# Group 8 of a linear recurrence loaded as one transfer per pair of sequences, and a drain without unread matmuls

## The chip, the cores and the metric

The kernel runs on one core of a Trainium2 chip. The metric is the device time of one execution in microseconds. A profile of one execution is shown beside the times; lines such as L252 are lines of the kernel's file. A core has a matrix engine (TensorE, PE in the profile), a vector engine (DVE), a scalar engine (ACT), GpSimd (POOL) and SyncE (SP), which issues most transfers. Transfers are moved by 16 DMA engines, which all issuers share.

## The reference

Four sequences of 5056 tokens with 256 channels go through a gated recurrence, and its output, taken as 20224 tokens, through a soft mixture of 8 experts with 4 slots each:

```python
sig = 1 / (1 + exp(-f_logit)); f = lower_bound + (1 - lower_bound) * sig
for t in range(S):                      # S = 5056, for each of B = 4 sequences
    h = f[:, t] * h + (1 - f[:, t]) * x[:, t]
    y[:, t] = h
logits = y.reshape(N, D) @ phi          # N = 20224, D = 256, 32 slots
slot_input = softmax(logits over tokens).T @ y
slot_out[e] = relu(slot_input[e] @ w1[e]) @ w2[e]      # F = 1024, 8 experts
out = softmax(logits over slots) @ slot_out
```

All inputs and the output are float32. Inputs f_logit and x are 20.7 MB each, w1 and w2 8.4 MB each, and the output is 20.7 MB.

## The kernel before

**Tiling.** The tokens of each sequence are cut into ten groups of G = 512. A unit is one group of one sequence, so there are 40. Groups 0 to 7 hold the first 4096 tokens. Group 9 is the last 512 tokens of the sequence, and group 8 (`odd` in the code) is what lies between: 448 tokens. Groups 2 to 7 are "long": there the two units of a pair are two successive groups of one sequence, loaded as one transfer of eight tokens on each of 128 partitions. In groups 0, 1, 8 and 9 the two units of a pair are the same group of two sequences. Units 32 to 35 are group 8: 32 and 33 are its first pair of sequences, 34 and 35 the second.

**One unit.** `load` brings f_logit into `f_t` and x into `x_t` (three buffers each, one pair in each buffer). `gate` (L241, scalar engine) makes `s_t`, the sigmoid of -f_logit in bf16. `enter` (L252, GpSimd) multiplies it by x into `u_t` (four buffers). Two neighbouring bf16 channels are then moved together as one float32 number: `s_to_channels` and `u_to_channels` transpose `s_t` and `u_t` on TensorE into PSUM (`sp`, `up`), so that channels lie on partitions and time runs along the row. `decay` (scalar engine) makes the decay factors `a`, `scan` (L319, vector engine) runs the recurrence, `to_tokens` and `keep_tokens` turn the result back into `ht`. `logits`, `exps`, `weights_to_tokens` and `slots` do the slots' softmax and sums.

**Group 8.** Its 448 tokens are not 4 x 128. Each sequence of a pair loads 3 tokens on each of 128 partitions (R3 = 3, 384 tokens), and the remaining L = 64 tokens of the two sequences come together on 128 partitions, alternating, as the fourth column of the pair's first half. That makes three transfers per tensor and pair (L222 and L226). `to_channels` turns the fourth column with an identity whose columns are split by sequence (L261) and the three others with one transpose each (L264). In the long groups `half_to_channels` (L273) turns a unit from one half of the partitions, with eight transposes of 64 partitions.

**Order.** The order is written out by hand in a loop over the units n (`manual_schedule`). Loads are issued six units ahead on SP's queue, every second unit; SP waits there for the buffer. On GpSimd the product of unit n + 3 is followed by weight loads as the table `W_AT` says. Weights are read as float32 and written as bf16 by transfers that GpSimd issues (L137, L147). Three of 16 loads are issued before unit 31; the others stand behind the products of units 34 to 37 and 39:

```python
W_AT = {9: 1, 17: 1, 25: 1, 31: 1, 32: 1, 33: 2, 34: 3, 36: 6}
```

The load of the last expert's w2 is issued in three parts.

**Drain.** After the last unit come the last slots (L461), `slot_sb` (the copy at L596), the slot input (L600), the experts' hidden layer (L631 to L664), the experts 0 to 3, then each further expert with its row sums (L670, L399), and the last expert (L725 to L740). Between these stand 24 matmuls whose results nobody reads: `spin` (L152, two of 128 columns) and `narrow` (L157, ten of 32 columns), once after the last slots and once after the slot input. Then the output is made from the stored exponentials and the slot outputs and written in transfers of up to 2 MB.

Of the kernel before, what the change touches and what calls it, by code (L numbers as in the profile page):

```python
# [9 lines left out]
F32 = mybir.dt.float32  # L10
# [8 lines left out]
def kernel(  # L19
# [10 lines left out]
    nc = tc.nc  # L30
    B, S, D = x.shape
    E = moe_w1.shape[0]
    F = moe_w1.shape[2]
    NS = moe_phi.shape[1]
    SPE = NS // E
    P = 128
    DC = D // P
    FC = F // P
    R = 4
# [6 lines left out]
    def first(g):  # L46
        return g * G if g < n_grp - 1 else S - G

    def used(g):
        return first(g + 1) - first(g) if g < n_grp - 1 else G  # L50
# [2 lines left out]
        return used(g) // R  # L53

    odd = n_grp - 2
    R3 = used(odd) // P
    L = used(odd) - P * R3
    assert 2 * L == P

    wide_r = 4 * R  # L60
    n_blk = (S // (P * wide_r))
# [1 line left out]
    blocks.append((n_blk * P * wide_r, (S - n_blk * P * wide_r) // P))  # L63
    assert sum(P * n_r for _, n_r in blocks) + L == S


    consts = ctx.enter_context(tc.tile_pool(name="consts", bufs=1))
    ident_f = consts.tile([P, P], F32, name="ident_f")
# [52 lines left out]
    rrow = store.tile([P, n_grp * R, B], F32, name="rrow")  # L121
    left = store.tile([P, L, 2], BF16, name="left")
    nc.vector.memset(left, 0.0)
# [8 lines left out]
    w1_sb = [wts.tile([P, DC, F], BF16, name=f"w1_sb{e}") for e in range(E)]  # L132
# [14 lines left out]
                nc.gpsimd.dma_start(out=w2_sb[i - E][:, ds(f, k)], in_=w2_r[i - E][:, ds(f, k)])  # L147


    def spin(dst, k, w):  # L150
        for _ in range(k):
            nc.tensor.matmul(dst[:, ds(0, w)], w1_sb[0][:, 0, :P], w1_sb[0][:, 0, :w],  # L152
                             start=True, stop=True, skip_group_check=True)

    def narrow(dst, k):
        for i in range(k):
            nc.tensor.matmul(dst[ds(i % B * NS, NS), ds(0, D)], w1_sb[0][:, 0, ds(0, NS)],  # L157
                             w1_sb[0][:, 0, ds(0, D)], start=True, stop=True,
                             skip_group_check=True)

    W_AT = {9: 1, 17: 1, 25: 1, 31: 1, 32: 1, 33: 2, 34: 3, 36: 6}
    w_next = [0]
    ctx.enter_context(tc.manual_schedule())
# [4 lines left out]
    with tc.tile_pool(name="sp2", bufs=3) as sp2, \  # L168
# [9 lines left out]
        slot_bank = pslot.tile([P, 2, D], F32, name="slot_ps")  # L178
# [12 lines left out]
        xs, fs, sts, uts, pss, psus, hs, hps, hts, lgs, ets = ({} for _ in range(11))  # L191

        def long(n):
            return 2 * B <= n < n_unit - 2 * B

        def place(n):
            if long(n):
                t, j = divmod(n, 2 * B)
                return 2 * t + j % 2, j // 2
            return divmod(n, B)  # L200
# [9 lines left out]
        def load(n, k=2):  # L210
            for src, dst, tag in ((f_logit, fs, "f_t"), (x, xs, "x_t")):
                if n % 2 == 0:
                    dst[n // 2] = ld.tile([P, 2, R, D], F32, name=tag, tag=tag)
                t = dst[n // 2]
                if long(n):
                    g, b = place(n)
                    nc.sync.dma_start(
                        out=t.rearrange("p u r d -> p (u r) d"),
                        in_=src[b, ds(first(g), 2 * G)].rearrange("(p r) d -> p r d", r=2 * R))
                elif n // B == odd:  # L220
                    b, t0 = n % B, first(odd)
                    nc.sync.dma_start(  # L222
                        out=t[:, 0, R3],
                        in_=src[ds(b, 2), ds(t0 + P * R3, L)].rearrange("b t d -> t b d"))
                    for m in range(2):
                        nc.sync.dma_start(  # L226
                            out=t[:, m, ds(0, R3)],
                            in_=src[b + m, ds(t0, P * R3)].rearrange("(p r) d -> p r d", r=R3))
                else:
                    for m in range(n, n + k):  # L230
                        nc.sync.dma_start(out=t[:, ds(m % 2, 1)], in_=tokens(src, m, 1))  # L231

        def gate(n, k=2):
            if n % 2 == 0:
                sts[n // 2] = sp2.tile([P, 2, R, D], BF16, name="s_t", tag="s_t")
            s_t, f_t = sts[n // 2][:, ds(n % 2, k)], fs[n // 2][:, ds(n % 2, k)]
            if n // B == odd:
                m = (R + R3) * D
                s_t = s_t.rearrange("p u r d -> p (u r d)")[:, :m]
                f_t = f_t.rearrange("p u r d -> p (u r d)")[:, :m]  # L240
            nc.scalar.activation(s_t, f_t, ACT.Sigmoid, scale=-1.0)  # L241

        def enter(n):
            uts[n] = sup.tile([P, R, D], BF16, name="u_t", tag="u_t")
            s_t, x_t = sts[n // 2][:, n % 2], xs[n // 2][:, n % 2]
            if n == 0:
                for r in range(0, R, 2):
                    nc.vector.tensor_tensor(uts[n][:, ds(r, 2)], s_t[:, ds(r, 2)],
                                            x_t[:, ds(r, 2)], ALU.mult)
            else:  # L250
                r = R3 if n // B == odd and n % 2 else R
                nc.gpsimd.tensor_tensor(uts[n][:, :r], s_t[:, :r], x_t[:, :r], ALU.mult)  # L252

        def to_channels(n, ps, t, rest):
            t = t.bitcast(F32)
            if n // B == odd:
                flat = ps.rearrange("c p r -> c (p r)")
                sides = ident_f.rearrange("p (t u) -> p u t", u=2)
                v = flat[:, ds(0, P * R3)].rearrange("c (p r) -> c p r", r=R3)
                k = P * R3 - n % 2 * L  # L260
                nc.tensor.matmul(flat[:, ds(k, P)], rest.bitcast(F32), sides,  # L261
                                 is_transpose=True, start=True, stop=True)
                for r in range(R3):
                    nc.tensor.transpose(v[:, :, r], t[:, r], ident_f)  # L264
                return
            for r in range(R):
                nc.tensor.transpose(ps[:, :, r], t[:, r], ident_f)  # L267

        def half_to_channels(n, ps, t):
            k = ds(n % 2 * (P // 2), P // 2)  # L270
            v = ps.rearrange("c p r -> c (p r)").rearrange("c (p r) -> c p r", r=2 * R)
            for r in range(2 * R):
                nc.tensor.transpose(v[:, :, r], t(r)[k].bitcast(F32), ident_f[k, k])  # L273

        def s_to_channels(n):
            if n % 2 == 0:
                pss[n // 2] = psp.tile([P, 2, P, R], F32, name="sp", tag="sp")
            to_channels(n, pss[n // 2][:, n % 2], sts[n // 2][:, n % 2],
                        sts[n // 2][:, 0, R3])

        def u_to_channels(n):
            ps = psu.tile([P, P, R], F32, name="up", tag="up")
            if long(n):
                half_to_channels(n, ps, lambda r: uts[n - n % 2 + r // R][:, r % R])
            else:
                to_channels(n, ps, uts[n], uts[n - n % 2][:, R3])
            psus[n] = ps.rearrange("c p r -> c (p r)").bitcast(BF16).rearrange(
                "c (t o) -> c t o", o=DC)

# [116 lines left out]
        def left_over():  # L406
            for b in range(B):
                k = ds(b * NS, NS)
                nc.gpsimd.tensor_copy(left[k, :, b % 2], etall[k, ds(S - L, L)])

# [74 lines left out]
        for n in range(n_unit):  # L485
# [14 lines left out]
            else:  # L500
# [40 lines left out]
                if n == n_unit - 2:  # L541
                    tail = psp.tile([P, 2, G], F32, name="tail", tag="sp")
# [46 lines left out]
        late_weights()  # L589
        slots(odd)  # L590
        late_slots()
        spin(tail[:, 1], 2, D)
        narrow(tail[:, 1], 10)
        slot_sb = hpool.tile([P, G, DC], BF16, name="slot_sb", tag="h")
        slot_sb = slot_sb.rearrange("p t o -> p (t o)").bitcast(F32)[:, ds(0, D)]
        nc.vector.tensor_copy(slot_sb, slot_ps)  # L596
# [2 lines left out]
        for o in range(DC):  # L599
            nc.tensor.matmul(sin_ps[:, o], slot_v[:, o], rep[:, 0],  # L600
                             start=True, stop=True, skip_group_check=True)
        spin(slot_bank[:, 1], 2, D)
        narrow(slot_bank[:, 1], 10)

    with tc.tile_pool(name="ew", bufs=1) as ew, \
         tc.tile_pool(name="pm", bufs=2, space=PSUM) as pm, \
# [17 lines left out]
        for q in range(E // Q):  # L624
            hi = ew.tile([P, F], BF16, name=f"hi{q}")
            for k in range(2):
                hi_ps = (psu.tile([P, H], F32, name="hi_ps", tag="up") if q == 0 else
                         pbig.tile([P, H], F32, name="hi_ps", tag=f"hi_ps{k}"))
                for o in range(DC):
                    for j in range(Q):  # L630
                        nc.tensor.matmul(hi_ps[ds(j * NS, NS)], sin[:, o],  # L631
                                         w1_sb[q * Q + j][:, o, ds(k * H, H)],
                                         start=(o == 0), stop=(o == DC - 1),
                                         skip_group_check=True)
# [7 lines left out]
        for q in range(E // Q):  # L642
# [4 lines left out]
            if q == 0:  # L647
                nc.tensor.matmul(cs_ps, rep2, cs1, start=True, stop=True)
            k = Q if q == 0 else Q - 1
            s0 = q * Q * SPE  # L650
            src = ht_ps[:, :, ds(s0, SPE)]
            src = bass.AP(tensor=src.tensor, offset=src.offset,
                          ap=[list(src.ap[0]), [P, FC], [NS + SPE, k], [1, SPE]])
            dst = hid[:, :, q * Q, ds(s0, SPE)]
            dst = bass.AP(tensor=dst.tensor, offset=dst.offset,
                          ap=[list(dst.ap[0]), [(E - 1) * NS, FC], [NS + SPE, k], [1, SPE]])
# [6 lines left out]
            src = ht_ps[:, :, ds((Q - 1) * NS + s0, SPE)]  # L663
# [23 lines left out]
        for i in range(0, n_late, 2):  # L687
            g_ps = (pbig.tile([P, 2, 2, P], F32, name="g_ps", tag="hi_ps1") if i else
                    psu.tile([P, 2, 2, P], F32, name="g_ps", tag="up"))
            for k in range(2):  # L690
                nc.tensor.matmul(g_ps[:, k], hi_v[tail_b, FC - n_late + i + k], ex[tail_b],
                                 start=True, stop=True, skip_group_check=True)
# [21 lines left out]
        for i in range(len(blocks)):  # L714
            expert(Q + i)
            row_sums(i)
            if i < len(blocks) - 1:
                k = ds(i * wide_r, wide_r)
# [3 lines left out]
        k = len(blocks) - 1  # L722
# [3 lines left out]
        for fc in range(FC):  # L726
# [4 lines left out]
                             start=fc == FC - n_late,  # L731
                             stop=fc in (FC - n_late - 1, FC - 1),
                             skip_group_check=True)
# [152 lines left out]
```

## Time and profile before

| | |
|---|---|
| median of 3 runs | 197.5 us (197.47 to 197.64) |
| the profiled execution | 197.47 us, span 195.7 us |
| PE busy | 147.1 us (75%) |
| DVE busy | 143.5 us (73%) |
| ACT busy | 141.4 us (72%) |
| POOL busy | 101.3 us (52%) |
| SP's transfers (q1) | 62.13 MB, 76.4% of 16 DMA engines |
| GpSimd's transfers (q0), bytes written | 8.42 MB, 21.6% |
| HBM read, written | 58.23 MB, 20.71 MB |

The span runs from the first to the last instruction; the rest of the execution's time lies around it. Busy times of different engines overlap. The page cuts the span into 40 slices of 4.9 us, and a digit there is a share in tenths. Issues from SP and GpSimd are marked SPq and POOLq in lists of waits.

### The profile page before, as it was taken

Reading aid. Unit: us, or ns where it says so; the run is one execution under the profiler, and the core shown is the slowest. Engines: PE = TensorE matmul, PEld = TensorE weight load, DVE = VectorE, ACT = ScalarE, POOL = GpSimd, SP = SyncE. Lnnn points to the kernel's source line nnn. Section 1 sums busy time; section 2 is a strip of 40 time slices with the busy share of each in tenths; the row PEclk is TensorE's granted clock in tenths of the full one; section 3 lists DMA queues with packets and bytes.
Section 4 is the critical chain, followed back from the end, with each engine's and each line's share of the span. In section 5 each row is a group of like instructions: output and inputs, shape, how many; then the busy total and the mean of one; then the engine's idle time right before and its main releaser. Section 6 shows DMA issues by size and latency. Waiting matters only on the chain.

```text
span 195.7 us, 3272 instructions
## 1 busy us (share of the span) xinstructions
PE 147.1 (75%) x1204; PEld 103.8 (53%) x1204; DVE 143.5 (73%) x185; ACT 141.4 (72%) x200; POOL 101.3 (52%) x78
## 2 busy tenths in 40 slices
PE   0688598897989979898997978996797999910000
PEld 0477478675767758665785857465564434300000
DVE  2669869989799999999999999442377998910000
ACT  3688688799799998899998798334089999940000
POOL 2589578874998688884969977280030000000000
PEclk9999889999999999999999999999999655555555
DMA  4999999999999999999999999999949999999994
GB/s 199 418 421 419 427 425 424 429 427 361 379 427 425 401 332 425 429 414 308 402 420 395 270 225 213 214 214 214 167 175 425 431 417 435 435 445 432 435 432 174
DMA packets 14161, 70.75 MB, mean 362 GB/s; under 512 B 1585, under 2 KB 2866, under 8 KB 10178
## 3 DMA queue, kind: packets, MB, share of 16 engines
q1 hardware_dynamic: 11520, 62.13, 76.4%
q0 software_dynamic: 2624, 8.42, 21.6%
q8 instruction: 9, 0.15, 0.3%
q14 instruction: 6, 0.05, 0.1%
q10 hardware_dynamic: 2, 0.00, 0.0%
HBM read 58.23 MB, written 20.71 MB: 403 GB/s over the span
## 4 chain that ended last, share of the span: by engine, by line
PE 24%; DMA 21%; DVE 15%; POOL 10%; ACT 9%; issue 6%; SPq 2%; POOLq 1%; ACTq 0%
DMA x_t<-in_x_dram 12%; DVE h L319 11%; DMA w_t<-in_moe_w_dram 10%; PE op L821 8%; POOL u_t L252 8%; ACT oc L762 5%; PE hp L332 4%; PE up L273 3%; PE sp L267 3%; DVE ht L351 3%; SPq L231 2%; PE slot_ps L189 2%; PE lg L365 1%; POOL w_sb L147 1%; ACT s_t L241 1%
## 5 line engine op out<-in xcount | busy, mean ns | idle before, releaser
L252 POOL TENSOR_TENSOR u_t<-s_t,x_t 128x1024 bf16<-128x1024 bf16 (+1 forms) x39 | 82.5, 2131 | 21.8 <-ACT s_t L241 15.1
L319 DVE TENSOR_TENSOR_SCAN h<-a,h,up 128x512 bf16<-128x512 f32 (+1 forms) x72 | 86.8, 1252 | 4.4 <-PE up L273 2.1
L241 ACT ACTIVATE s_t<-f_t 128x2048 bf16<-128x2048 f32 (+2 forms) x23 | 38.3, 1668 | 6.4 <-DMA f_t<-in_f_logit_dram 6.4
L332 PE MATMUL hp<-ident_f,h 128*128 128x128 f32 (+1 forms) x160 | 29.6, 309 | 8.0 <-DVE ht L351 6.0
L332 PEld LDWEIGHTS hp<-ident_f,h 128*128 128x128 f32 (+1 forms) x160 | 23.2, 207 | 19.1 <-DVE ht L351 12.4
L267 PE MATMUL sp<-ident_f,s_t 128*128 128x128 f32 x144 | 22.3, 300 | 5.6 <-ACT s_t L241 3.8
L301 ACT ACTIVATE a<-sp,lbs 128x1024 f32<-128x1024 bf16 x24 | 25.5, 1115 | 0.6 <-PE sp L267 0.6
L762 ACT ACTIVATE oc<-op,rrow 128x256 f32<-128x256 f32 x62 | 24.2, 551 | 0.1
L821 PE MATMUL op<-slot_bd,etall 64*128 64x512 bf16 x62 | 22.8, 570 | 0.6 <-POOL slot_bd L751 0.2
L267 PEld LDWEIGHTS sp<-ident_f,s_t 128*128 128x128 f32 x144 | 18.0, 154 | 7.7 <-ACT s_t L241 4.6
L308 ACT ACTIVATE a<-sp,lbs 128x512 f32<-128x512 bf16 (+2 forms) x22 | 17.9, 859 | 4.7 <-PE sp L267 4.3
L758 DVE TENSOR_TENSOR oc<-op,rrow 128x512 f32<-128x512 f32 x31 | 19.7, 685 | 1.6 <-PE op L821 1.5
L273 PE MATMUL up<-ident_f,u_t 64*128 64x64 f32 x192 | 17.8, 230 | 2.2 <-POOL u_t L252 2.1
L273 PEld LDWEIGHTS up<-ident_f,u_t 64*128 64x128 f32 x192 | 14.0, 138 | 6.2 <-POOL u_t L252 2.8
L189 PE MATMUL slot_ps<-rep,ident_f 128*128 128x256 f32 x52 | 16.7, 415 | 0.0
L821 PEld LDWEIGHTS <-etall 64*128 64x128 bf16 x62 | 9.1, 154 | 13.4 <-issue 8.0
L351 ACT COPY ht<-hp 128x512 f32<-128x512 f32 (+1 forms) x20 | 11.7, 583 | 3.5 <-PE hp L332 3.4
L351 DVE COPY ht<-hp 128x512 f32<-128x512 f32 (+1 forms) x20 | 13.3, 667 | 0.8 <-PE hp L332 0.8
L319 DVE TENSOR_TENSOR_SCAN h<-a,up 128x512 bf16<-128x512 f32 x8 | 9.3, 1209 | 2.4 <-PE up L267 2.4
L267 PE MATMUL up<-ident_f,u_t 128*128 128x128 f32 x48 | 9.4, 327 | 0.5 <-POOL u_t L252 0.5
L365 PE MATMUL lg<-h,phi 128*32 128x512 bf16 (+1 forms) x80 | 9.4, 389 | 0.3 <-ACT et L389 0.2
L189 PEld LDWEIGHTS slot_ps<-rep,ident_f 128*128 128x128 f32 x52 | 8.3, 194 | 1.6 <-issue 0.6
(127 smaller groups left out, 141.9 us busy)
## 6 DMA issues: line engine op xcount, KB each, us to landing
f_t<-in_f_logit_dram SPq DMA_DIRECT2D x12, 1024.0 KB, 12.3
x_t<-in_x_dram SPq DMA_DIRECT2D x12, 1024.0 KB, 12.0
out_dram<-oc SPq DMA_DIRECT2D x6, 2048.0 KB, 14.1
w_sb<-in_moe_w_dram POOLq DMA_DIRECT2D x14, 512.0 KB, 11.0
f_t<-in_f_logit_dram SPq DMA_DIRECT2D x12, 512.0 KB, 8.4
x_t<-in_x_dram SPq DMA_DIRECT2D x12, 512.0 KB, 9.9
out_dram<-oc SPq DMA_DIRECT2D x4, 896.0 KB, 6.4
out_dram<-ob SPq DMA_DIRECT2D x1, 2048.0 KB, 9.7
```

Of the source, the lines that this page charges most:

```text
L189: nc.tensor.matmul(slot_bank[:, 1], ident_f, wide_rep, start=False, stop=False, skip_group_check=True)
L241: nc.scalar.activation(s_t, f_t, ACT.Sigmoid, scale=-1.0)
L252: nc.gpsimd.tensor_tensor(uts[n][:, :r], s_t[:, :r], x_t[:, :r], ALU.mult)
L267: nc.tensor.transpose(ps[:, :, r], t[:, r], ident_f)
L273: nc.tensor.transpose(v[:, :, r], t(r)[k].bitcast(F32), ident_f[k, k])
L301: nc.scalar.activation(a, sp[:, :, :, :, o], ACT.Identity, scale=nomlb[:, ds(o, 1)], bias=1.0)
L319: nc.vector.tensor_tensor_scan(h[:, :T, o], decays[n // 2, o][:, n % 2, :T], up[:, :T, o], hs[number(g - 1, b)][:, ds(used(g - 1) - 1, 1), ...
L332: nc.tensor.transpose(hp[:n_p, r], hw[:, :n_p, r], ident_f)
L351: copy(hts[g][:n_p, b].rearrange("p r d -> p (r d)").bitcast(F32), hps.pop(n)[:n_p].rearrange("p r c -> p (r c)"))
L758: nc.vector.tensor_tensor(ob, op, scale.broadcast_to(list(ob.shape)), ALU.mult)
L762: nc.scalar.activation(ob[:, i], op[:, i], ACT.Copy, scale=scale[:, i])
L821: nc.tensor.matmul(op.rearrange("p u d -> p (u d)"), ew[:, :, r], slot_bd[ds(j * 2 * NS, 2 * NS)].rearrange("s u d -> s (u d)"), start=Tru ...
```

## The change

Group 8 of a pair of sequences now comes in one transfer per tensor: seven tokens on each of 128 partitions, the first sequence on partitions 0 to 63 and the second on 64 to 127. The tile is read as one row of 7 x 256 numbers. `gate` covers the same 1792 numbers as before, and `enter` of the pair's first unit covers four of the seven columns, of the second three. Both units are turned by halves, with seven transposes of 64 partitions each, as the long units' `u_t` were. In the drain, `spin` and `narrow` and their calls are gone.

```diff
-    R3 = used(odd) // P
-    L = used(odd) - P * R3
-    assert 2 * L == P
+    L = P // 2
+    R7 = used(odd) // L
+    assert used(odd) == L * R7 and R < R7 < 2 * R
...
-    def spin(dst, k, w):
...
-    def narrow(dst, k):
...
                 elif n // B == odd:
-                    b, t0 = n % B, first(odd)
                     nc.sync.dma_start(
-                        out=t[:, 0, R3],
-                        in_=src[ds(b, 2), ds(t0 + P * R3, L)].rearrange("b t d -> t b d"))
-                    for m in range(2):
-                        nc.sync.dma_start(
-                            out=t[:, m, ds(0, R3)],
-                            in_=src[b + m, ds(t0, P * R3)].rearrange("(p r) d -> p r d", r=R3))
+                        out=t.rearrange("p u r d -> p (u r d)")[:, ds(0, R7 * D)],
+                        in_=src[ds(n % B, 2), ds(first(odd), L * R7)].rearrange(
+                            "b (p r) d -> b p (r d)", r=R7))
...
-                m = (R + R3) * D
+                m = R7 * D
...
-                r = R3 if n // B == odd and n % 2 else R
+                r = R7 - R if n // B == odd and n % 2 else R
...
-        def half_to_channels(n, ps, t):
-            k = ds(n % 2 * (P // 2), P // 2)
-            v = ps.rearrange("c p r -> c (p r)").rearrange("c (p r) -> c p r", r=2 * R)
-            for r in range(2 * R):
+        def half_to_channels(n, ps, t, n_r):
+            k = ds(n % 2 * L, L)
+            v = ps.rearrange("c p r -> c (p r)")[:, ds(0, L * n_r)].rearrange(
+                "c (p r) -> c p r", r=n_r)
+            for r in range(n_r):
                 nc.tensor.transpose(v[:, :, r], t(r)[k].bitcast(F32), ident_f[k, k])
...
+            ps, t = pss[n // 2][:, n % 2], lambda r: sts[n // 2][:, r // R, r % R]
+            if n // B == odd:
+                half_to_channels(n, ps, t, R7)
+            else:
+                to_channels(n, ps, t)
...
+            t = lambda r: uts[n - n % 2 + r // R][:, r % R]
+            if long(n) or n // B == odd:
+                half_to_channels(n, ps, t, 2 * R if long(n) else R7)
             else:
-                to_channels(n, ps, uts[n], uts[n - n % 2][:, R3])
+                to_channels(n, ps, t)
...
-        spin(tail[:, 1], 2, D)
-        narrow(tail[:, 1], 10)
...
-        spin(slot_bank[:, 1], 2, D)
-        narrow(slot_bank[:, 1], 10)
```

## The prediction

> **What bounds the kernel now.** I read the page's slices first, then the timeline of GpSimd and of TensorE up to the drain, then the page's queues and issues. The slices (4.9 us each) give the busy share of the DMA engines and what they moved:
>
> ```profile
> DVE  2669869989799999999999999442377998910000
> DMA  4999999999999999999999999999949999999994
> GB/s 199 418 421 419 427 425 424 429 427 361 379 427 425 401 332 425 429 414 308 402 420 395 270 225 213 214 214 214 167 175 425 431 417 435 435 445 432 435 432 174
> ```
>
> The DMA row is 9 from 5 us to 140 us, dips for one slice, and is 9 again while the output goes out. The drop to 213 GB/s at 112 to 140 us is no idle time: there the weights come, float32 read and bf16 written, and the written bytes are counted. So the kernel is a row of transfers without a gap, a short drain between 139.5 and 145 us, and the output. The vector engine is nearly as busy until 120 us, but from then on only weights decide. From the timeline (start, us, engine, line, operation, in brackets the idle time before it and who ended it), GpSimd first, then TensorE:
>
> ```profile
> 100.89 2.15 POOL L252 TENSOR_TENSOR u_t<-s_t,x_t 128x1024 bf16<-128x1024 bf16 x1 [1.49 <-PE up L273]
> 102.99 0.59 POOL L137 DMA_DIRECT2D w_sb<-in_moe_w_dram  x1
> 103.60 1.68 POOL L252 TENSOR_TENSOR u_t<-s_t,x_t 128x768 bf16<-128x768 bf16 x1
> ...
> 118.39 2.18 POOL L147 DMA_DIRECT2D w_sb<-in_moe_w_dram  x4
> ```
>
> ```profile
> 137.10 0.40 PE L670 MATMUL sum_ps<-w_sb,hid 128*32 128x256 bf16 x8 [0.89 <-DMA w_sb<-in_moe_w_dram]
> ...
> 139.52 0.40 PE L670 MATMUL sum_ps<-w_t,hid 128*32 128x256 bf16 x8 [0.87 <-DMA w_t<-in_moe_w_dram]
> ```
>
> To be seen: GpSimd issues the weights between its products (`enter`), in order. The product at 100.89 is unit 34, the first of the second pair of group 8 (the 768-wide one after it is unit 35), and 13 of the 16 weight loads stand behind it. Matmuls of the experts then wait for one weight load after another, 2.4 us apart. The end follows the last weights: 139.5 us to the end of the span at 195.7 is 56.2 us of drain and output. Whatever occupies a DMA engine before 139.5 us moves the end by as much, unless other DMA engines can take the work.
>
> Third, how transfers are spread over the 16 DMA engines: the page's queues (packets, MB, share of 16 DMA engines' time) and issues (count, KB each, us to landing):
>
> ```profile
> q1 hardware_dynamic: 11520, 62.13, 76.4%
> ...
> q10 hardware_dynamic: 2, 0.00, 0.0%
> ...
> f_t<-in_f_logit_dram SPq DMA_DIRECT2D x4, 384.0 KB, 10.4
> x_t<-in_x_dram SPq DMA_DIRECT2D x4, 384.0 KB, 8.6
> ...
> f_t<-in_f_logit_dram SPq DMA_DIRECT2D x2, 128.0 KB, 10.0
> x_t<-in_x_dram SPq DMA_DIRECT2D x2, 128.0 KB, 9.4
> ...
> lb_row<-in_lower_bound_dram ACTq DMA_DIRECT2D x1, 1.0 KB
> ```
>
> q1 is SP's queue. Its 80 issues have 128 rows each, and 11520 is exactly 80 x (128 + 16): 128 data packets and 16 further ones per issue, one closing packet for each DMA engine. q10 holds one issue, the single row of `lb_row`: 2 packets, 1 + 1, so one DMA engine. The count of DMA engines is thus not always 16; it depends on how the transfer is laid out. All 80 issues lead with a dimension of 128, or of 64 (the 128 KB pieces, written `b t d -> t b d` with the 64 tokens ahead of the pair); `lb_row` leads with 1.
>
> **The change, part by part.** *The load.* Twelve issues for group 8 (four of 128 KB, eight of 384 KB, 3.67 MB) become four of 128 rows x 7168 B. Their source is written `b (p r) d -> b p (r d)`: it leads with the pair, a dimension of 2, with 64 rows under it. No row of the trace shows a leading 2. The bounds are 16 DMA engines (as with 64 and 128) and one (as with `lb_row`, leading 1). A split that cuts the leading dimension gives 2 here, 64 there (capped at 16) and 1 for `lb_row`; it fits every row, and a leading 2 is much nearer to 1 than to 64. I take 2.
>
> What no run here has shown, a page states: the Trainium skill, DMA: Bandwidth & Descriptors, section "Why a DMA increments its semaphore by 16 and not by 1", says that the descriptor generator takes each side's slowest dimension above one and uses the largest number up to 16 that divides both, which is 2 for this load. The same page's rules for kernel authors speak the other way, for one large transfer over 128 partitions in place of several; the second rival is what that would give.
>
> The price: one DMA engine carries 425 GB/s / 16 = 26.6 GB/s by the full slices, 26.0 by the queue row (62.13 MB over 76.4% of 16 x 195.7 us). Half a load is 64 x 7168 B = 0.459 MB, which is 17.3 to 17.7 us; I take 17.5. The four loads queue behind each other on the same two DMA engines: 70.0 us. Before, each of the 16 spent 9.0 us on group 8 (3.67 MB at the 408 GB/s that the windows from 94 to 98 us show). Net on the two: +61.0 us, and the other 14 have nothing to give, since every later transfer, weights too, needs its share from all 16.
>
> Step by step: the first of these loads starts at about 87 us (issued at 78.6, its pieces landed 10 us later). One weight load falls among them (issued at 85.8, 0.52 MB written at 213 GB/s, 2.5 us). The last x half lands at 87 + 2.5 + 70.0 = 159.5 us, where unit 34's product had started at 100.89. Behind that product wait the 13 weight loads (6.8 MB, 32.0 us), and on the two DMA engines the last group's 4.19 MB (9.9 us): 201.4 us. The same sum for the kernel before (2.5 + 9.0 + 9.9 + 32.0 from 87) gives 140.4, and the weights really ended at about 141.5; so 61 us later, at 202.5.
>
> Does compute keep up? From unit 34's product to the first expert matmul (131.92) took 31.0 us; from 159.5 that is 190.5, ahead of the fifth expert's weights (134.66 + 61 = 195.7). But the last group's loads now alternate with weights on the two DMA engines, so the last products come nearer to 183 than to 179, and the 13.5 us from the last product (118.4) to the experts (131.9) end at about 197. That is 1 us late, and the 0.9 us waits per expert make up part of it: 0 to 2.5, I take +0.5.
>
> *The turning by halves.* Per unit and tensor, 4 transposes of 128 (one 0.28 and three 0.49 in the timeline, 0.60 from first to last end) become 7 of 64 (eight took 0.70, so 0.61): nothing, and TensorE waits for others there anyway. `u_to_channels` of the first unit of a pair now also needs the second unit's product: 1.68 us and a weight issue of 0.59 later on GpSimd. Queued behind that transpose are the scans of unit 34 on the vector engine. Before, product 35 ended at 105.3 and the transposes of unit 34 ran at 107.6, so it hides; after, it falls in the wait above. The gate (1792 wide) and the products (1024 and 768) keep their sizes.
>
> *The issues.* Eight fewer on SP, some 0.5 us each: SP waits for buffers far longer, so nothing.
>
> *The unread matmuls.* 24 go (0.27 us each, 1.8 us in all, at 126.5 to 127.3 and 127.8 to 128.6). The copy of `slot_ps` ended at 127.05 and the matmul behind the first burst started at 127.26, so at most 0.2 us of path, ahead of weights that come last: nothing. What they could hold up is the granted clock, which the windows from 40 to 150 us give as 1.00. Bounds: nothing, or all TensorE work of the drain's chain (139.5 to 142.6, 3.0 us) at half clock, +3.0. I take 0: in 135 to 140 us TensorE was busy 3.2 of 5 us without any such matmul, and the clock held.
>
> The Trainium skill, TensorE: Matmul & The Clock Gate, Part 1, says that an idle window of about 3.4 us halves the clock; the waits of 17 us between the new loads would then show as 5s in the PEclk row, and the sum would be 3 us higher if the drain too began at half clock.
>
> Sum against the profiled execution (197.47 us, span 195.7; the median of the runs is 197.5): 197.47 + 61.0 + 0.5 = 259.0.
>
> **The rivals.** *Two DMA engines (forecast), 259.0.* Against it: no row has a leading 2. Price ends: 63 us if a lone DMA engine moves 29 GB/s, so 251; and 17.7 per half, +2.5 for compute and +3 for the clock, with a few us of lost overlap, 270.
>
> *Sixteen after all, ending on the other side.* If the rows are spread by the 128 partitions of the destination, group 8 takes 3.67 MB at 427 GB/s, 8.6 in place of 9.0 us, because 1 KB and 3 KB rows become 7 KB ones: 197.1, faster by 0.2%, with the clock's 3.0 against it. For it: every q1 issue so far used 16. It decides if the closing packets of each new load number 16.
>
> *One DMA engine:* four times 35 us, less 9.0: 328. `lb_row` is the only case for it.
>
> *Four or eight,* if the 64 under the 2 is split too: 35 or 17.5 in place of 70, so 224 or 206. Nothing shows such a split.
>
> **How the numbers follow.** Two 0.90, sixteen 0.07, the others 0.03. The range is the forecast's own, 250 to 270; it leaves out the other cases and the ends of its own. A measurement here tells 0.2% from no change. Sixteen gives faster 0.04 and same 0.03; the rest is slower, 0.93.
>
> **What would show it.** q1 should have 68 x 144 + 4 x 130 = 10312 packets (10368 if sixteen). From about 92 to 159 us the DMA row should fall to 1 and GB/s to about 53, with DVE, ACT and POOL mostly idle and the four loads landing some 17 us after each other. The scalar engine's gate of unit 32 should wait some 15 us for `f_t`, and unit 34's product should start near 160. The stretch from the last weights to the end should still be 56 us. If GB/s stays above 400 through 90 to 100 us, the forecast is wrong.

## The result, and the profile after

The changed kernel takes 261.4 us (median of 6 runs, 260.8 to 262.5) where the kernel before, beside it, takes 197.6 us (197.5 to 197.9): 1.323 times as long, with an interval of 1.320 to 1.327. The profiled execution took 262.5 us with a span of 260.8 us, 65.1 us more than that of before; the times of the profile below are those of this execution. A slice of the page is now 6.5 us. First the rows that answer to those of before, then the queues:

```profile
DVE  3698999899999990051000430039933398884000
PEclk9999999799999996555555555559999775555555
DMA  6999999999999811111116744599999189999995
GB/s 253 421 420 427 420 435 421 342 426 429 350 412 426 253 45 54 54 53 54 53 54 185 219 132 130 147 195 212 210 214 199 33 345 428 430 442 425 420 442 246
...
q1 hardware_dynamic: 10312, 62.13, 59.0%
...
q10 hardware_dynamic: 2, 0.00, 0.0%
```

From 91 to 137 us (slices 15 to 21) the DMA row reads 1, and GB/s, from 98 us on, 53 or 54, twice 26.6: two DMA engines work and fourteen are idle. q1 has 10312 packets, which is 68 x 144 + 4 x 130, so each of the four new loads closes with 2 packets and not 16. The bytes are the same as before, 62.13 MB. DVE is at 0 from 98 to 143 us but for a 5 and a 1, where the first pair's units run.

Who waits, from the list of waits (engine, tile, line, releaser: idle us, number of waits, longest):

```profile
ACT s_t L226 <- DMA f_t<-in_f_logit_dram: 71.9, 13, 31.2
POOL u_t L237 <- DMA x_t<-in_x_dram: 70.5, 10, 36.3
```

The scalar engine's gate and GpSimd's product each wait some 70 us in all for their loads. Where these waits lie is in the timelines, of the scalar engine, of GpSimd and of TensorE (the product is L237 now, the experts' row sums L645):

```profile
107.35 1.70 ACT L226 ACTIVATE s_t<-f_t 128x1792 bf16<-128x1792 f32 x1 [13.95 <-DMA f_t<-in_f_logit_dram]
...
143.22 1.70 ACT L226 ACTIVATE s_t<-f_t 128x1792 bf16<-128x1792 f32 x1 [31.21 <-DMA f_t<-in_f_logit_dram]
```

```profile
124.60 3.73 POOL L237 TENSOR_TENSOR u_t<-s_t,x_t 128x1024 bf16<-128x1024 bf16 x2 [28.81 <-DMA x_t<-in_x_dram]
...
164.67 2.13 POOL L237 TENSOR_TENSOR u_t<-s_t,x_t 128x1024 bf16<-128x1024 bf16 x1 [36.34 <-DMA x_t<-in_x_dram]
166.74 0.58 POOL L137 DMA_DIRECT2D w_sb<-in_moe_w_dram  x1
```

```profile
201.85 0.47 PE L645 MATMUL sum_ps<-w_sb,hid 128*32 128x256 bf16 x8 [0.88 <-DMA w_sb<-in_moe_w_dram]
...
204.29 0.62 PE L645 MATMUL sum_ps<-w_t,hid 128*32 128x256 bf16 x8
```

Each of the four group 8 loads releases one instruction: gate of unit 32 at 107.4, product of unit 32 at 124.6, gate of unit 34 at 143.2, product of unit 34 at 164.7. They come 17 to 21 us apart. The weight issue that stood behind the product at 103.0 now stands at 166.7, and the expert matmul that was at 139.52 (expert 6, counted from 0) is at 204.29. From there to the end of the span it is 56.5 us, nearly as before (56.2).

### The profile page after: what moved, and what is told of

It is laid out like the page before. It is cut to its first block, busy times and chain, and to the rows that moved or that the text cites. A ratio compares the mean times of both kernels' runs of the same rounds, so it can differ in the third digit from the quotient of the medians.

```text
span 260.8 us, 3261 instructions
## 1 busy us (share of the span) xinstructions
PE 156.8 (60%) x1204; PEld 109.5 (42%) x1204; DVE 144.2 (55%) x185; ACT 141.8 (54%) x200; POOL 101.2 (39%) x78
## 3 DMA queue, kind: packets, MB, share of 16 engines
q1 hardware_dynamic: 10312, 62.13, 59.0%
## 4 chain that ended last, share of the span: by engine, by line
DMA 41%; another core or an unknown queue 15%; PE 13%; ACT 5%; POOL 5%; DVE 5%; SPq 4%; issue 3%; POOLq 0%; ACTq 0%; DVEq 0%
DMA x_t<-in_x_dram 17%; DMA f_t<-in_f_logit_dram 17%; DMA w_t<-in_moe_w_dram 7%; PE op L796 7%; SPq L216 4%; POOL u_t L237 4%; DVE h L298 4%; ACT oc L737 3%; PE op L743 1%; PE up L248 1%; PE hp L311 1%; ACT ht L330 1%; POOL w_sb L147 1%; ACT a L280 1%
## 5 line engine op out<-in xcount | busy, mean ns | idle before, releaser
L237 POOL TENSOR_TENSOR u_t<-s_t,x_t 128x1024 bf16<-128x1024 bf16 (+1 forms) x39 | 82.5, 2126 | 87.6 <-DMA x_t<-in_x_dram 70.5
L311 PE MATMUL hp<-ident_f,h 128*128 128x128 f32 (+1 forms) x160 | 31.7, 327 | 63.5 <-ACT ht L330 58.5
L311 PEld LDWEIGHTS hp<-ident_f,h 128*128 128x128 f32 (+1 forms) x160 | 24.8, 210 | 75.1 <-ACT ht L330 62.0
L796 PE MATMUL op<-slot_bd,etall 64*128 64x512 bf16 x62 | 23.5, 587 | 0.4 <-POOL slot_bd L726 0.3
L248 PE MATMUL up<-ident_f,u_t 64*128 64x64 f32 x220 | 22.0, 244 | 2.4 <-POOL u_t L237 2.4
L241 PEld LDWEIGHTS sp<-ident_f,s_t 128*128 128x128 f32 x144 | 18.2, 155 | 7.9 <-ACT s_t L226 4.1
L248 PEld LDWEIGHTS up<-ident_f,u_t 64*128 64x128 f32 x220 | 17.7, 151 | 7.2 <-issue 3.0
L178 PE MATMUL slot_ps<-rep,ident_f 128*128 128x256 f32 x52 | 19.3, 470 | 1.0 <-POOL rep L86 1.0
L178 PEld LDWEIGHTS slot_ps<-rep,ident_f 128*128 128x128 f32 x52 | 9.1, 212 | 3.4 <-POOL rep L86 1.2
L344 PE MATMUL lg<-h,phi 128*32 128x512 bf16 (+1 forms) x80 | 10.2, 412 | 0.2
```

The source lines that it names most:

```text
L178: nc.tensor.matmul(slot_bank[:, 1], ident_f, wide_rep, start=False, stop=False, skip_group_check=True)
L241: nc.tensor.transpose(ps[:, :, r], t(n % 2 * R + r).bitcast(F32), ident_f)
L311: nc.tensor.transpose(hp[:n_p, r], hw[:, :n_p, r], ident_f)
L796: nc.tensor.matmul(op.rearrange("p u d -> p (u d)"), ew[:, :, r], slot_bd[ds(j * 2 * NS, 2 * NS)].rearrange("s u d -> s (u d)"), start=Tru ...
```

## The experiments

All medians are beside runs of the kernel before on the same chip, 197.5 to 197.7 us each time.

**The number of DMA engines alone.** The same four loads, with 64 ahead of the pair instead of 2. The source's order is the only thing edited: the partitions then hold rows of the two sequences in turn, while the kernel still turns them by halves, so group 8's tokens are mixed up.

```diff
-                            "b (p r) d -> b p (r d)", r=R7))
+                            "b (p r) d -> p b (r d)", r=R7))
```

> The changed kernel with one thing turned round: the source of group 8's load is written with the 64 row-blocks ahead of the pair (64, 2, 1792) in place of (2, 64, 1792). Same four issues, same bytes, same 7168 B rows, same turning by halves; the two sequences of a pair then alternate on the partitions, so group 8's tokens are mixed up and only the time is read. Theory S (a transfer is cut along its leading dimension, over the largest number of DMA engines up to 16 that divides it): all 16 DMA engines, q1 has 72 x 144 = 10368 packets, no stretch at 53 GB/s, 197.0 to 198.0 us. Rival T (the single transfer, the 7 KB rows or the turning by halves costs the time): stays above 250 us.

Measured: 197.16 us (197.0 to 198.4, 12 runs), ratio 0.997 (0.995 to 0.999). From its page:

```profile
GB/s 198 422 418 419 435 429 419 426 426 357 376 426 428 407 331 424 426 426 342 392 416 396 262 221 215 215 214 215 158 183 429 427 417 439 433 439 433 436 433 178
...
q1 hardware_dynamic: 10368, 62.13, 76.6%
```

10368 is 72 x 144: sixteen closing packets per load, and no slice at 53. Bytes, buffers, gate, products and transposes are those of the changed kernel, and its whole loss is gone. The order of two dimensions of the source is the cause. It also bounds the rest of the change: the larger loads, the turning and the missing unread matmuls together cost nothing here.

**The rule with other numbers.** Four engines: each new load takes 32 rows from each of the four sequences, so the leading dimension is 4. The tokens of group 8 are mixed by this.

```diff
+                    q = n % B // 2
...
-                        in_=src[ds(n % B, 2), ds(first(odd), L * R7)].rearrange(
-                            "b (p r) d -> b p (r d)", r=R7))
+                        in_=src[:, ds(first(odd), L * R7)].rearrange(
+                            "b (p q r) d -> q b p (r d)", q=2, r=R7)[q])
```

> The changed kernel with the same four loads of 128 rows x 7168 B, each now from all four sequences, 32 rows of each (4, 32, 1792), so that only the leading dimension goes from 2 to 4; group 8's tokens then stand at other places, so only the time is read. Theory S: 4 DMA engines, 32 rows each, 32 x 0.273 us = 8.75 us per load and 35.0 us for four in place of 9.0: about 26 us above the kernel before, 223 to 227 us, q1 68 x 144 + 4 x 132 = 10320 packets, and about 107 GB/s in the stretch of these loads. Rival T: about 261 us.

Measured: 232.2 us (one run), 10320 packets on q1.

```profile
134.82 2.13 POOL L238 TENSOR_TENSOR u_t<-s_t,x_t 128x1024 bf16<-128x1024 bf16 x1 [18.21 <-DMA x_t<-in_x_dram]
```

10320 is 68 x 144 + 4 x 132: four closing packets, as the rule has it. The time missed what was expected: the product of unit 34 came at 134.8, where the sum (87 + 2.5 + half of 70.0) gives 124.5. The lone DMA engines took longer than their bytes say: the packets of the four loads add up to 43.1 us on each of the four in place of 35.0, and 88 of the third load's 128 took over 0.35 us. The experiment on group 9 below takes this up.

And in the kernel before, only the four 128 KB pieces with the pair ahead:

```diff
-                        in_=src[ds(b, 2), ds(t0 + P * R3, L)].rearrange("b t d -> t b d"))
+                        in_=src[ds(b, 2), ds(t0 + P * R3, L)].rearrange("b t d -> b t d"))
```

> The kernel before with one thing turned round: the four 128 KB pieces of group 8 are read with the pair ahead of the 64 tokens (2, 64, 256) in place of (64, 2, 256); the tokens of the two sequences then stand in halves where the kernel takes them as alternating, so only the time is read. Theory S: these four small transfers go over 2 DMA engines, 64 x 1 KB each, 2.5 us at 26 GB/s, 10.0 us for four in place of 0.6: 206 to 209 us, q1 76 x 144 + 4 x 130 = 11464 packets. Rival T (only a large single transfer costs): 197.5 us and 11520 packets.

Measured: 207.0 us (one run) and 11464 packets, 76 x 144 + 4 x 130. So the packets follow the leading dimension for 1 KB rows too. Half a megabyte that goes through two DMA engines costs this kernel 9.5 us.

**A way around it with the data in place.** Each load as two, one per sequence, 64 rows onto 64 partitions:

```diff
-                    nc.sync.dma_start(
-                        out=t.rearrange("p u r d -> p (u r d)")[:, ds(0, R7 * D)],
-                        in_=src[ds(n % B, 2), ds(first(odd), L * R7)].rearrange(
-                            "b (p r) d -> b p (r d)", r=R7))
+                    for m in range(2):
+                        nc.sync.dma_start(
+                            out=t.rearrange("p u r d -> p (u r d)")[ds(m * L, L), ds(0, R7 * D)],
+                            in_=src[n % B + m, ds(first(odd), L * R7)].rearrange(
+                                "(p r) d -> p (r d)", r=R7))
```

> The changed kernel with each of group 8's loads issued as two, one per sequence, each 64 rows x 7168 B onto 64 partitions (leading dimension 64); the result is the reference's. Theory S: 16 DMA engines, q1 has 68 x 144 + 8 x (64 + 16) = 10432 packets, 197.0 to 198.5 us. Rival P (each DMA engine has a door of its own into a part of the partitions, and 16 DMA engines writing onto 64 partitions share half of the doors): the 7 KB packets take up to twice as long, group 8 costs up to 17 us in place of 9, up to 206 us. Rival T: stays above 250 us.

Measured: 205.4 us (204.8 to 206.8, 6 runs), ratio 1.039 (1.034 to 1.043). From its page:

```profile
GB/s 214 418 421 419 431 426 426 425 426 320 425 425 423 345 400 423 428 210 244 261 238 382 341 262 220 214 212 216 207 81 391 426 448 413 439 439 413 449 429 213
...
q1 hardware_dynamic: 10432, 62.13, 77.5%
...
f_t<-in_f_logit_dram SPq DMA_DIRECT2D x4, 448.0 KB, 17.1
...
x_t<-in_x_dram SPq DMA_DIRECT2D x4, 448.0 KB, 16.6
```

10432 is 68 x 144 + 8 x 80, so all sixteen DMA engines take part. Still the rate is 210 to 261 GB/s in the four slices from 86 to 107 us, and a 7168-byte packet took 0.468 us (median of group 8's loads) against 0.272 in the changed kernel, and 0.272 too with 64 ahead, where all sixteen also carry these loads at once. 3.67 MB at 240 GB/s instead of 408 is 15.3 instead of 9.0 us, 6.3 of the 7.8 us lost. Using all DMA engines isn't enough: loads onto half of the partitions ran at little more than half the rate. The Trainium skill, DMA: Bandwidth & Descriptors, section "The descriptor swizzle", gives partitions 0 to 63 and 64 to 127 different ports into the memory, eight for each half; halved rates fit that, but no run here shows a port by itself.

**What group 9 does to the lone DMA engines.** The changed kernel, with group 9's loads cut to a quarter: one of four columns is loaded, and gate and product read it four times.

```diff
-                        nc.sync.dma_start(out=t[:, ds(m % 2, 1)], in_=tokens(src, m, 1))
+                        c = 1 if n // B == last else R
+                        nc.sync.dma_start(out=t[:, ds(m % 2, 1), ds(0, c)],
+                                          in_=tokens(src, m, 1)[:, :, ds(0, c)])
...
+                    f_m = f_t[:, m, ds(0, 1)].broadcast_to([P, R, D])
+                    nc.scalar.activation(s_t[:, m], f_m, ACT.Sigmoid, scale=-1.0)
...
+                x_r = x_t[:, ds(0, 1)].broadcast_to([P, R, D]) if n // B == last else x_t[:, :r]
```

> The changed kernel with thin loads of group 9: 1 KB on each of 128 partitions in place of 4 KB, and gate and products read that quarter four times over (group 9's results are not the reference's; only the time is read). Everything up to the last load of group 8 is unchanged. Theory K (the last x load of group 8 took 21.4 us in place of 17.4 because the other 14 DMA engines brought group 9 at the same time and packets got in each other's way): unit 34's product starts at 160.2 to 161.2 us in place of 164.7. Rival L (late issue or a slower transfer of its own): it stays at 164 to 165. The whole gets 4 us (K) shorter plus up to 7 us, the three quarters of group 9 that the two DMA engines no longer carry: 250 to 255 us, by L 254 to 258.

Measured: 254.7 us (one run). That lies in the ranges of both theories; unit 34's product decides between them.

```profile
160.38 2.14 POOL L245 TENSOR_TENSOR u_t<-s_t,x_t 128x1024 bf16<-128x1024 bf16 x1 [31.59 <-DMA x_t<-in_x_dram]
```

Unit 34's product comes 4.3 us earlier than in the changed kernel (164.67), although its own four loads are untouched, as K has it. The packets say where. The 128 packets of a load of group 8, divided among two DMA engines, add up to 17.7, 17.4, 18.3 and 21.9 us per DMA engine in the changed kernel, and to 18.0, 17.4, 17.4 and 18.2 us here. Of the last load's packets 42 took over 0.35 us there (the longest 0.587), and 8 did here. Two stretches of the changed kernel show the neighbours (stretch, its length, busy us and count on PE, PEld, DVE, ACT and POOL, granted clock, DMA share, GB/s):

```profile
124.60:136.00 11.40, 0.00 (x0) 0.00 (x0) 0.00 (x0) 0.00 (x0) 3.73 (x2) 0.50 0.13 53
136.00:164.00 28.00, 7.95 (x46) 5.31 (x46) 5.06 (x5) 3.98 (x4) 0.00 (x0) 0.50 0.54 159
```

Up to 136 us the two work alone at 53 GB/s. Then the other fourteen bring group 9, 159 GB/s in all, and the packets of the two slow down. That group 9's loads are the cause is shown by cutting them; what in them slows the two is not.

**The unread matmuls, in the kernel before.** Only the calls are left out:

```diff
-        spin(tail[:, 1], 2, D)
-        narrow(tail[:, 1], 10)
...
-        spin(slot_bank[:, 1], 2, D)
-        narrow(slot_bank[:, 1], 10)
```

> The kernel before without the 24 unread matmuls of the drain, all else as it was. Prediction's term: nothing, 197.3 to 197.8 us, the granted clock 1.0 through the drain. Rival C (they hold up the clock): a stretch of 3.4 us at half clock falls into the drain (120 to 145 us) and the time rises by 0.3 to 3 us.

Measured: 198.92 us (198.4 to 200.1, 12 runs), ratio 1.006 (1.004 to 1.009): 1.3 us slower. Its stretches, then those of the experiment with 64 ahead, which has no unread matmuls either, then the one of the kernel before:

```profile
127.00:130.40 3.40, 2.83 (x28) 1.42 (x32) 0.74 (x5) 0.88 (x2) 2.83 (x3) 0.69 1.07 214
144.00:147.40 3.40, 3.04 (x19) 1.96 (x18) 3.40 (x7) 3.40 (x10) 1.13 (x2) 1.00 0.41 136
```

```profile
127.00:130.40 3.40, 2.83 (x28) 1.37 (x32) 0.75 (x5) 0.88 (x2) 3.17 (x4) 0.74 1.06 212
144.00:147.40 3.40, 3.14 (x16) 1.78 (x15) 3.40 (x7) 3.40 (x11) 0.82 (x1) 0.75 0.98 364
```

```profile
144.00:147.40 3.40, 3.04 (x19) 1.85 (x17) 3.40 (x7) 3.40 (x10) 1.07 (x2) 1.00 0.89 327
```

The granted clock does fall without them, to 0.69 and 0.74 around 128 us. But that isn't the loss. The kernel with 64 ahead has the same dip and loses nothing, and without the calls expert 6's matmul (139.62 against 139.52) and the slot outputs (142.64 against 142.57) are within 0.1 us; the weights come later than the slow matmuls. The loss lies after. From SP's first issue of output (143.44 before, 143.55 without the calls) to the end of the span it is 52.2 us before and 53.7 without; in the other eleven profiles of this case it is 52.0 to 52.2, also in the two kernels whose clock dipped to half in the drain (64 ahead and the changed kernel). Between 144 and 147.4 us the output moves at 136 GB/s, with the granted clock at 1.00, instead of at 327 and 364. The view of the DMA engines over 143 to 148 us, in slices of 0.125 us, has this:

```profile
DMA  0000000000069947993000003001000399999999
...
q8 instruction: 1, 0.02, 1.8%
```

The output starts at 144.4 and almost stops from 145.4 to 147. A transfer of 16 KB on the queue of instructions begins at 144.6 and takes 1.45 us, so it ends inside that gap. SP's issues of this output took longer by as much as was lost; first without the calls, then in the kernel before:

```profile
144.47 3.93 SPq L791 DMA_DIRECT2D out_dram<-ob  x5
```

```profile
144.36 2.59 SPq L795 DMA_DIRECT2D out_dram<-ob  x5
```

The first of the five alone took 1.98 us, from 144.47 to 146.45, in place of 0.41. In the kernel before the instruction transfer begins at 142.6, in the one with 64 ahead at 142.1: between the last weights and the first output, where nothing else moves.

If the place follows from how many instructions TensorE has run by then, any matmuls will do, wherever they stand. Two experiments put 24 back elsewhere. The first keeps `spin` and moves all 24 to the step of unit 20 (they write into the bank that also holds the slots' sums, and the slot inputs aren't those of the reference then); the second takes 24 tiny ones of two columns:

```diff
+                if n == 20:
+                    spin(slot_bank[:, 1], 24, NS)
```

> The kernel before with its 24 unread matmuls moved out of the drain to unit 20 (32 columns each), so that the drain has none, but TensorE's program is as long as before when it gets there. Without them the time was 198.9 us, and a 16 KB transfer on the queue q8 (instructions) that had run at 142.6 us, between weights and output, ran at 144.6 us into the first output. Theory F (what costs is this transfer's new place, set by the count of instructions): it runs near 142.6 us again and the time is 197.4 to 197.9 us, though the clock may still drop at 128 to 132 us. Rival C (the clock's drop in the drain costs): 198.5 to 199.2 us.

```diff
+                if n in (18, 20, 22):
+                    for _ in range(8):
+                        nc.tensor.matmul(slot_bank[ds(0, NS), 1, ds(0, 2)], ident_f[:, ds(0, NS)],
+                                         ident_f[:, ds(0, 2)], start=False, stop=False,
+                                         skip_group_check=True)
```

> The kernel before without the 24 unread matmuls of the drain, and with 24 tiny matmuls (32 x 2) at units 18, 20 and 22, into the bank half that nobody reads: TensorE has 1204 matmuls as before, 1180 without them. Theory F (what cost 1.3 us without the unread matmuls is the place of the 16 KB instruction transfer): it runs at 142 to 143 us, the first output is not held up, 197.3 to 197.9 us, also if the clock drops at 128 us. Rival C (the clock's drop in the drain costs): 198.5 to 199.2 us if the clock drops there.

Measured: 197.60 us (12 runs, ratio 1.001, 0.999 to 1.002) and 197.56 us (12 runs, ratio 1.0005, 0.999 to 1.002). The transfer begins at 142.6 and 141.6 us. So 24 matmuls far ahead of the drain give the 1.3 us back. In both the clock stayed at 1.00 in the drain, for reasons that weren't followed up, so of the two explanations these runs alone can't choose. The place of the loss does, and the kernel with 64 ahead, which had the dip and not the loss: the clock's dip is out. That the instruction transfer is what holds SP's issue rests on the one kernel where the two meet, and on its going away in these two.

**The unread matmuls, in the changed kernel.** The calls (and their two helpers) are put back, once by themselves and once beside a second measurement of the changed kernel:

```diff
+        spin(tail[:, 1], 2, D)
+        narrow(tail[:, 1], 10)
...
+        spin(slot_bank[:, 1], 2, D)
+        narrow(slot_bank[:, 1], 10)
```

> The changed kernel with the 24 unread matmuls back in the drain. The prediction's term for them is nothing: 261.0 to 261.9 us. Rival C (they hold the clock): the 3.4 us at half clock at 202 us are gone and 0.3 to 1 us with them, 260.4 to 261.1. In both cases group 8's load costs the same 64 us.

> The changed kernel once more, to stand beside the next one on the same chip: 261.0 to 262.0 us.

> The changed kernel with the 24 unread matmuls back, on the same chip as the run ahead of it. Prediction's term: no difference, within 0.4 us. Rival C (they hold up the clock): 0.3 to 1 us faster than the changed kernel. Theory F (their 48 instructions move the instruction transfers, here to 205.8 us, which holds nothing up): no difference.

Measured: 262.61 us (4 runs) with them at first; then, side by side, 262.71 without (262.0 to 262.8, 5 runs) and 262.48 with (261.5 to 263.9, 6 runs). Side by side that is no difference, with ranges that overlap. The first 262.61 lies above both of its expected ranges, but so does the changed kernel itself in its second measurement (262.71, where 261.0 to 262.0 was expected and the first gave 261.43), so only the pair side by side can be compared. In the changed kernel the 24 that go and the 24 transposes that come leave TensorE at 1204 matmuls, as before, and its instruction transfer begins at 207.2 us, ahead of the output's start at 208.5.

## Why the prediction was right, and where it was off

*Two DMA engines.* The step that decided, from closing packets and `lb_row` alone, is shown from both sides: 10312 packets and 53 GB/s as forecast, and the loss gone when 64 stands ahead. Leads of 2, 4 and 64 gave 2, 4 and 16 closing packets. This is the rule of the Trainium skill, DMA: Bandwidth & Descriptors, section "Why a DMA increments its semaphore by 16 and not by 1", and the trace agrees; that page's advice of one large transfer over 128 partitions, the second rival, held only with the 64 ahead, as its rule of a multiple of 16 outermost, in the same table, would have it.

*The price, +61.0.* This is the term that was mis-sized. The four loads were put at 4 x 17.5 = 70.0 us, each as if alone. They measured 17.7 + 17.4 + 18.3 + 21.9 = 75.3. The stations show where it enters:

| | forecast | measured |
|---|---|---|
| gate of unit 32 | 107.0 | 107.35 |
| product of unit 32 | 124.5 | 124.60 |
| gate of unit 34 | 142.0 | 143.22 |
| product of unit 34 | 159.5 | 164.67 |

(The two in the middle are 87 + 2.5 + 35.0 and + 52.5 by the same sum, the first + 17.5.) Two loads went as forecast; the other two ran while fourteen DMA engines brought group 9, and with a quarter of group 9 the four loads took 71.0 and the product came at 160.38. The prediction had a "lost overlap" of a few us only in its upper bound. Its lower end of 251 took 29 GB/s for a lone DMA engine, which no row had; 7168 bytes in 0.272 us are 26.4.

*After the product.* The weights behind it and the last group were to end 61.5 us later than before; expert 6's matmul came 64.8 us later (204.29 for 139.52). Of the 5.2 us above the forecast at the product, 1.9 were thus made up on the way. Which part of the queue sum was too high there, no run tells.

*Compute, +0.5.* From unit 34's product to that matmul it took 38.6 us before and 39.6 after: +1.0. That holds the last group's loads, which were split off in the sum, so it isn't the same quantity, but inside the bounds of 0 to 2.5.

*The drain.* From that matmul to the slot outputs 3.05 us before and 3.40 after, because the stretch from 202 to 205.5 us ran at half clock: in the profile of its second measurement the same kernel had the clock at 1.00 there and took 3.07 (204.09 to 207.16). So this dip comes and goes with one and the same program. PEclk fell to 5 in the waits, as the second page that the prediction drew on has it (the Trainium skill, TensorE: Matmul & The Clock Gate, Part 1), and was back at 9 from 176 to 202 us. Of the +3.0 at half clock, 0.35 came.

*Turning by halves and issues, 0.* Right: the kernel with 64 ahead has the same count of transposes and the same four loads and takes 197.16, where the rival with sixteen DMA engines was put at 197.1.

*Unread matmuls, 0.* The number was right for the changed kernel and the reason incomplete. Leaving them out costs 1.3 us in the kernel before; the bounds of 0 to +3.0 looked at the clock, while the time was lost in the first output. In the changed kernel the 24 new transposes bring TensorE's matmuls back to 1204; that this is why nothing was lost there is inferred.

In sum, 262.5 for the profiled execution against 259.0: +5.2 at the product, -1.9 on the way, +0.35 in the drain, and -0.1 behind the slot outputs. The profiled execution is the slowest of the six; their median of 261.4 is 2.4 above the forecast.

## What to carry to other kernels

Write a transfer so that its slowest dimension is a multiple of 16 (2 and 4 gave two and four DMA engines here, 64 and 128 all sixteen), and read from the closing packets of its queue how many DMA engines it has; a load onto 64 partitions with all of them is no full replacement. A transfer on few DMA engines costs its bytes on those alone for all that waits behind it, and more once others move loads beside it. Where a few matmuls in the drain seem to matter, look where the instruction transfers fall before blaming the clock.

## What the runs showed of the hardware that was not expected

- Sixteen DMA engines writing onto 64 partitions: 0.468 us per packet of 7168 bytes instead of 0.272, some 240 GB/s instead of 408.
- A packet of 7168 bytes on one of two lone DMA engines took 0.272 us while the other fourteen were idle, and up to 0.587 us while they moved group 9. With 64 ahead, where all sixteen carried group 8 at once, the median was 0.272 too, so busy neighbours alone don't explain it; the reason stays open.
- The issuing engine was held too. SP's timeline (start, us, line) of the changed kernel, where a row of one or two issues took 0.3 to 1.5 us in the kernel before:

```profile
84.45 19.63 SPq L210 DMA_DIRECT2D f_t<-in_f_logit_dram  x1
104.21 16.78 SPq L210 DMA_DIRECT2D x_t<-in_x_dram  x1
121.09 18.65 SPq L216 DMA_DIRECT2D f_t<-in_f_logit_dram  x2
140.27 5.96 SPq L216 DMA_DIRECT2D x_t<-in_x_dram  x2
```

  SP is busy with one issue after another from 84 to 146 us, with gaps of about half a microsecond at most. Group 9 (L216), issued at 94.5 before, gets its turn at 121.1, and its first two issues end at 139.7; the fourteen idle DMA engines had nothing to move before, because its issues stood behind those of group 8. That a full queue is what holds SP is argued from the times, not shown by a run.
- A transfer of 16 KB of instructions began at 144.6 us in place of 142.6 when 24 matmuls were left out, met the first output, and the kernel took 1.3 us longer. That the length of the program places it, and that it is what held SP's issue for 1.98 us, is inferred from these kernels, not measured by itself.
- No kernel here that computes the reference was faster than the one before. The kernel with 64 ahead is 0.3% below it, but with group 8 mixed; whether a way to turn that layout with the sequences apart keeps the 0.3% wasn't tried.
